# Row normalisation shared with GpSimd, 16-bit angles and filter loads ahead of the rows in a fused convolution and MLP kernel

## Chip, cores and metric

One core of a Trainium2 chip runs the kernel. The metric is the device time of one execution in microseconds (us). The span that a profile shows runs from the first to the last instruction and is some 2 us shorter. The runs come in a fast and a slow state; only fast runs are compared here. The granted clock is the share of TensorE's full clock that the chip allowed, 1.0 being all of it. Ratios are the mean time of one kernel's fast runs over that of the other's fast runs of the same rounds, so they differ a little from the ratio of the medians that are quoted.

## The reference, cut to what matters

```python
x = A_q                                          # (1, 2048, 640) bf16
g = sigmoid((x * gate_w).sum(-1))
# A: short causal convolution of k (4 taps per channel), times v,
#    then a convolution of length 2048 with ssm_k per channel through an FFT
kv = k_shift * v
y  = irfft(rfft(pad(kv)) * rfft(pad(ssm_k)))[:2048] + kv * ssm_D
a  = x * y
# B: row-normalised x, mixed over the rows by a two-layer MLP
h  = (x - mean(x)) / sqrt(var(x) + 1e-5)         # mean and var over the 640 channels
u  = gelu(einsum("bsd,sf->bdf", h, w1) + b1)
b  = (einsum("bdf,fs->bds", u, w2) + b2).transpose()
out = g * a + (1 - g) * b
```

## The kernel before: the parts that matter

The kernel turns the FFTs into products with sine tables on TensorE, in four residue classes of rows (`p` = 0 to 3), and mixes them by additions on VectorE. It does not issue its operations in the order of its text. It gives every operation an assumed duration, plans all engines with a list scheduler and emits each engine's operations in the planned order. An engine then takes its list strictly in that order.

```python
def ts(eng, o, a, s1, s2, op0, op1=None, mode=1, prio=None, extra=0.0):   # tensor_scalar
    n = n_of(o)
    d = dve_dur(n, mode) + extra if eng == "DVE" else n / 900.0 + 0.2     # GpSimd: 0.91 us for 640
    ...
def ln_scale(a, b):                       # 1/sqrt(var+eps) of tiles a..b-1, on GpSimd
    ts("POOL", sd[:, a:b], mv[:, a:b, 1], 1e-5, None, ALU.add, prio=0)
    tt("POOL", rstd[:, a:b], sd[:, a:b], V(cst, 1, [[0, n]]), ALU.pow, prio=0).dur = 1.05
    return tt("POOL", sd[:, a:b], sd[:, a:b], rstd[:, a:b], ALU.mult, prio=0)
def ln_apply(a, b):                       # (x - mean) * rstd in place, on VectorE
    for t in range(a, b):
        ts("DVE", xs, xs, mv[:, t, 0:1], rstd[:, t:t + 1], ALU.subtract, ALU.mult, mode=4, ...)
```

Here `ts` is an operation with one tensor and scalar operands, `tt` one with two tensors, `act` one of ScalarE. An evacuation copies TensorE's products out of PSUM, the memory where they land. I call `ln_scale` of tiles 0 to 7 the first scale and of tiles 8 to 15 the second.

A row tile is 128 rows of 640 channels. There are 16. TensorE's first MLP layer reads the normalised tiles; it serves as fill wherever the convolution makes TensorE wait. The order around the normalisation, the loads and the evacuation of the transposed filter were:

```python
for a, b in SSM0[:2]: ssm_load(0, a, b)          # filter blocks 0..3 of the first half
x_load(0)                                        # rows
ssm_load(0, *SSM0[2])                            # last filter block
for hk in range(1, 4): x_load(hk)
...
# filter block transposed on TensorE, D folded in by a 1-row matmul, evacuated by ScalarE
act(V(wT, ...), PSUM, ACT.Copy, name="wT")
...
for t in range(12): ln_tile(...)                 # statistics (bn_stats) on VectorE
ln_scale(0, 8);  ln_apply(0, 8)
for t in range(12, 16): ln_tile(...)             # after the first normalisations
ln_scale(8, 16); ln_apply(8, 16)
for g0 in KFP: tt("POOL", KF[...], cw, m32, ALU.mult)   # tap products, 4 pieces, on GpSimd
k_turn(0); k_turn(1)                             # reorder k (VectorE copies kp<-kn)
mixing(C[0], SS, 0)                              # first VectorE mixing of the filter spectrum
```

Of the kernel before, what the change touches and what calls it, by code (L numbers as in the profile page):

```python
# [9 lines left out]
BF16 = mybir.dt.bfloat16  # L10
F32 = mybir.dt.float32
I32 = mybir.dt.int32
ACT = mybir.ActivationFunctionType
# [5 lines left out]
class _Tracker:  # L19
# [31 lines left out]
    def regions(self, ap):  # L51
        name = ap.tensor.name
        info = self.mem.get(name)
        if info is None:
            return []
        space, base, rowsize, esize = info
        apl = [tuple(p) for p in ap.ap]
        esz_ap = mybir.dt.size(ap.dtype)
        assert esz_ap == esize, "bitcast size change unsupported in tracker"
        off = ap.offset  # L60
        assert isinstance(off, int)
        pstride, pcount = apl[0]
        if pcount > 1:
            assert pstride == rowsize, (name, apl, rowsize)
        p0 = off // rowsize
        rem = off % rowsize
        p1 = p0 + pcount
        assert p1 <= 128
        free = apl[1:]
        outer = free[:-1]  # L70
        inner = free[-1:] if free else []
        nouter = 1
        for st, ct in outer:
            nouter *= ct
        res = []
        if outer and nouter <= 64:
            idxs = [0] * len(outer)
            for _ in range(nouter):
                o = rem
                for (st, ct), i in zip(outer, idxs):  # L80
                    o += st * i
                lo = o
                hi = o
                for st, ct in inner:
                    ext = st * (ct - 1)
                    if ext < 0:
                        lo += ext
                    else:
                        hi += ext
                hi += 1  # L90
                assert lo >= 0 and hi <= rowsize, (name, apl, off, rowsize)
                res.append(self._reg(space, p0, p1, base + lo * esize, base + hi * esize))
                for d in range(len(outer) - 1, -1, -1):
                    idxs[d] += 1
                    if idxs[d] < outer[d][1]:
                        break
                    idxs[d] = 0
        else:
            lo = rem
            hi = rem  # L100
            for st, ct in free:
                ext = st * (ct - 1)
                if ext < 0:
                    lo += ext
                else:
                    hi += ext
            hi += 1
            assert lo >= 0 and hi <= rowsize, (name, apl, off, rowsize)
            res.append(self._reg(space, p0, p1, base + lo * esize, base + hi * esize))
        return res  # L110
# [172 lines left out]
    def mm(self, ps_ap, lhsT, rhs, start, stop, final_val, inc, transpose=False):  # L283
# [11 lines left out]
        ins = self.nc.tensor.matmul(ps_ap, lhsT=lhsT, rhs=rhs, start=start, stop=stop, skip_group_check=True)  # L295
# [30 lines left out]
class _Sched:  # L326
# [59 lines left out]
    def run(self):  # L386
# [13 lines left out]
        free = {e: 2.4 if e == "ACT" else 0.0 for e in engs}  # L400
        port = {"DVE": 0.0, "POOL": 0.0}
        dma_free = 0.0
# [109 lines left out]
def _build(nc, A_q, A_k, A_v, A_shift_k, A_ssm_k, A_ssm_D, B_x, B_w1, B_b1, B_w2, B_b2, gate_w, out):  # L512
# [10 lines left out]
    with ExitStack() as es:  # L523
# [61 lines left out]
        acol = alloc("acol", [128, 2, 4], I32, at=base_of(SS))  # L585
        brow = alloc("brow", [128, 2, 128], I32, at=base_of(SS) + 64)
# [9 lines left out]
        ksh = [alloc(f"ksh{i}", [128, 4, D], BF16, at=base_of(GT) + 5120 * (1 + i)) for i in range(2)]  # L596
        rows = alloc("rows", [20, 5, 512], BF16, at=base_of(GT))
        kn = [alloc(f"kn{i}", [128, 4, D], BF16, at=base_of(ring[1]) + 5120 * i) for i in range(2)]
        kp = [alloc("kp0", [128, NG, 128], BF16, at=base_of(ring[1]) + 10240), alloc("kp1", [128, NG, 128], BF16, at=base_of(GTB))]
        pint = alloc("pint", [128, 4, 2, 2, 256], I32, at=base_of(ring[1]))  # L600
# [83 lines left out]

        def memset(eng, ap, val, prio=None):
            return SC.add(eng, 0.2, lambda s: T.op(eng, lambda e: e.memset(ap, val), [], [ap]), [], [ap], prio=prio)  # L686
# [41 lines left out]

        def ssm_load(h, a, b):
            dma(ssm[:, a:b, 1024 * h:1024 * h + 1024], dr(A_ssm_k, 128 * S * a + 1024 * h, [[S, 128], [128 * S, b - a], [1, 1024]]), 128 * (b - a) * 2048, chain=True, rate=(262.0 if a == 0 else 195.0) if h == 0 else 385.0)  # L730
# [7 lines left out]
        def x_load(hk):  # L738
            dma(X[:, hk, :, :], dr(A_q, 512 * hk * D, [[4 * D, 128], [1, 4 * D]]), 128 * 5120, chain=True, rate=410.0)
# [30 lines left out]
        for a, b in SSM0[:2]:  # L770
            ssm_load(0, a, b)
        x_load(0)
        ssm_load(0, *SSM0[2])
# [11 lines left out]
        SPIN = (7, 3, 3, 2, 2)  # L785

        def spin(k):
            return [((lambda s: s[:, 0:512]), zz[:, 0:128], zz[:, :], True, True)] * k
# [4 lines left out]
        iota = lambda ap, pat, b, cm: SC.add("POOL", 0.2, lambda s: T.op("POOL", lambda e: e.iota(ap, pat, base=b, channel_multiplier=cm), [], [ap]), [], [ap])  # L793
        iota(dif[:, :], [[1, 128]], 0, -1)
        iota(acol[:, :, :], [[4, 2], [1, 4]], 0, 8)
        iota(brow[:, :, :], [[-512, 2], [4, 128]], 1, 0)
        iota(dif2[:, :], [[1, 32]], 128, -1)
        ts("DVE", ident[:, :], dif[:, :], 0.0, None, ALU.is_equal)
        memset("POOL", rows[0:20, 3:5, :].rearrange("g a b -> g (a b)")[:, 0:896], 0.0)
        ro, ri = V(rows, 1536, [[128, 4], [160, 4], [1, 32]], pn=20), V(rows, 0, [[1, 4], [0, 4], [4, 32]], pn=20)  # L800
        SC.add("DVE", 0.6, lambda s: T.op("DVE", lambda e: e.tensor_copy(ro, ri), [ri], [ro]), [ri], [ro], prio=0, name="taps")
        PORD = (0, 2, 1, 3)
        sins = {}
        for p in PORD:
            pv = pint[:, p, :, 1, :]
            t_ = tt("DVE", pv, V(acol, p, [[4, 2], [0, 256]]), V(brow, 0, [[0, 2], [1, 256]]), ALU.mult, mode=1)
            ts("DVE", pint[:, p, :, 0, :], pv, 1024.0, None, ALU.add, mode=2)
            pa = pint[:, p, :, :, :].rearrange("q a b c -> q (a b c)")
            if p != 0:
                t_.after.add(pprev)  # L810
            pprev = ts("DVE", pa, pa, 4095, None, ALU.bitwise_and, mode=2)
            pv3 = pa
            sins[p] = act(FTB[:, p, :, :, :, :].rearrange("q a b c d -> q (a b c d)"), pa, ACT.Sin, bias=cst[:, 0:1],
                scale=-(2.0 * math.pi / 4096.0) * (1.0 - 1e-6), name="sin")

# [24 lines left out]

        def transp(h, db):
            vt = _VT("cv")
            items = []
            for kt in range(2):
                for p in range(4):
                    o = (lambda s, j=4 * kt + p: s[:, 128 * j:128 * j + 128])
                    dfold = h == 0 and kt == 0 and p == 0
                    if dfold:
                        items.append((o, ident[0:1, :], Drow[0:1, 128 * db:128 * db + 128], True, False))
                    items.append((o, V(ssm, db * S + 1024 * h + 4 * kt + p, [[8, 128]]), ident[:, :], not dfold, True))  # L850
            m_ = mms(vt, (spin(SPIN[db]) if h == 0 else []) + items, name="wtr")
            m_.dur = 0.5
            o_ = act(V(wT, 2 * h * SL + 128 * db, [[SL, 2], [D, 4], [1, 128]]), (lambda s: s[:, :].rearrange("q (a b c) -> q a b c", a=2, b=4)), ACT.Copy, vt=vt, name="wT")
            if h == 0:
                o_.after.add(sins[0 if db == 0 else 2])
# [85 lines left out]
        MIXP = 330  # L941
        LNA = 8
        lnlast = []
        kfirst = []
        KFP = (0, 5, 10, 15)
        srcW = lambda h: (lambda kt, p, ci: wT[:, 2 * h + kt, p, 320 * ci:320 * ci + 320])
        for h in range(2):
            for db in range(ND):
                transp(h, db)
            if h == 0:  # L950
                consts()
            if h in (1,):
                fwd_even(srcW(h), h, C[h], 1.0 / 1024.0, h == 1, "W")
            for p in (PORD if h not in (1,) else PORD[2:]):
                if h == 0 and p in (1, 3):
                    sins[p].prio = SC.ops[-1].idx - (16.5 if p == 1 else 8.5)
                fwd(srcW(h), h, p, C[h], p, 1.0 / 1024.0, "W", (lambda c, k2: False) if h == 0 else (lambda c, k2: c == 1))
            if h == 0:
                for t in range(8):
                    ln_tile(t // 4, t % 4)  # L960
                for t in range(8, 12):
                    ln_tile(t // 4, t % 4)
                lnlast.append(SC.ops[-1])
                ln_scale(0, LNA)
                ln_apply(0, LNA)
                lnlast.append(SC.ops[-1])
                for t in range(12, 16):
                    for o_ in ln_tile(t // 4, t % 4):
                        o_.after.update(lnlast[-1:])
                ln_scale(LNA, 16)  # L970
                ln_apply(LNA, 16)
                lnlast.append(SC.ops[-1])
                for g0 in KFP:
                    tt("POOL", KF[:, g0:g0 + 20 // len(KFP), :, :], V(cw, 7 * g0, [[7, 20 // len(KFP)], [1, 7], [0, 32]]), V(m32, 0, [[0, 20 // len(KFP)], [0, 7], [1, 32]]), ALU.mult, xr=[pv3] if g0 == 0 else []).after.update(kfirst[:1])
# [344 lines left out]
```

## Time and profile before

| what | before |
|---|---|
| time, median of 3 (range) | 181.99 us (181.78 to 183.0) |
| span of the profiled run, granted clock | 179.7 us, 1.0 |
| first block of filter products on TensorE | 13.18 us |
| first MLP product on TensorE | 21.02 us |
| end of the last statistics on VectorE | 27.97 us |
| first mixing addition on VectorE | 32.94 us |

In later batches on other chips the kernel before took 181.98 to 182.46 us (medians of 7 to 11). In a timeline line the numbers are start, length, engine and kernel line; "x8" counts instructions run together; the bracket tells how long the engine was idle before it and what it waited for.

### The profile page before, as it was taken

To read this page: it belongs to the slowest core of one execution; us is meant where nothing else is said; L and a number is where in the kernel's file an instruction comes from. 1 tells how busy PE (TensorE), PEld (TensorE's weight loads), DVE (VectorE), ACT (ScalarE), POOL (GpSimd) and SP (SyncE) were. 2 spreads that over 40 slices of the span, in tenths; PEclk is the share of its full clock that TensorE was granted. 3 is DMA by queue.
4 is the path that set the end of the run, shared out by engine and by line. 5 is a ranking of instruction groups with operands and counts; after the bars stand their busy time and mean duration, and the time that the engine had idled before them with its cause. 6 is when DMAs were issued, how large, how long until landed. Compare 5 with 4: busy or idle time off the path is not lost.

```text
span 179.7 us, 3335 instructions
## 1 busy us (share of the span) xinstructions
PE 173.1 (96%) x1381; PEld 128.7 (72%) x1381; DVE 171.2 (95%) x203; ACT 116.9 (65%) x176; POOL 43.7 (24%) x42
## 2 busy tenths in 40 slices
PE   7969998899999999999999999999999999999993
PEld 2546785587778777776777778888888887777772
DVE  7999895999999999999999899999999999999984
ACT  5899998899898999617999932131231323753760
POOL 4089404190000054000240010402525000252000
PEclk9999999999999999999999999999999999999999
DMA  6999999999999999998299969797999999599463
GB/s 151 381 411 372 388 294 194 268 420 296 212 258 286 184 271 248 229 228 218 60 243 299 197 94 365 170 225 253 166 193 217 210 200 385 218 154 240 116 233 135
DMA packets 38542, 43.51 MB, mean 242 GB/s; under 512 B 15867, under 2 KB 31360, under 8 KB 38528
## 3 DMA queue, kind: packets, MB, share of 16 engines
q1 hardware_dynamic: 33296, 32.16, 58.2%
q0 software_dynamic: 5200, 11.14, 35.6%
q8 instruction: 11, 0.18, 0.4%
q14 instruction: 3, 0.02, 0.0%
q10 hardware_dynamic: 32, 0.01, 0.0%
HBM read 25.87 MB, written 2.62 MB: 159 GB/s over the span
## 4 chain that ended last, share of the span: by engine, by line
PE 88%; ACT 10%; DVE 0%; issue 0%
PE pp L295 88%; ACT wT L670 3%; ACT C L670 2%; ACT ksh L670 2%; ACT FTB L670 2%; ACT L670 1%; ACT GT L670 0%; DVE O L682 0%; DVE zz L686 0%; ACT cw L670 0%; DVE cst L686 0%
## 5 line engine op out<-in xcount | busy, mean ns | idle before, releaser
L295 PE MATMUL pp<-X,ring 128*128 128x320 bf16 x384 | 55.6, 299 | 0.0
L626 DVE TENSOR_TENSOR C<-C 128x2560 bf16<-128x2560 bf16 (+2 forms) x37 | 54.5, 1521 | 0.0
L295 PE MATMUL pp<-GT,W 128*128 128x320 bf16 x384 | 52.6, 299 | 0.0
L295 PEld LDWEIGHTS pp<-GT,W 128*128 128x128 bf16 x384 | 43.6, 114 | 8.6
L295 PEld LDWEIGHTS pp<-X,ring 128*128 128x128 bf16 x384 | 37.1, 98 | 14.9 <-DVE X L641 0.7
L670 ACT ACTIVATE C<-pp 128x640 bf16<-128x640 f32 x64 | 40.4, 723 | 4.9 <-PE pp L295 4.9
L670 ACT ACTIVATE O<-pp,c,omg 128x640 bf16<-128x640 f32 x15 | 13.3, 884 | 34.7 <-PE pp L295 34.7
L264 POOL DMA_DIRECT2D C<-C x8 | 10.9, 1610 | 41.7 <-DVE C L626 38.3
L295 PE MATMUL pp<-wT,FTB 128*128 128x320 bf16 x112 | 17.2, 299 | 2.5 <-ACT wT L670 1.4
L670 ACT ACTIVATE cgb<-pp,gg 128x640 bf16<-128x640 f32 x16 | 12.7, 794 | 5.7 <-PE pp L295 5.3
L295 PEld LDWEIGHTS pp<-wT,FTB 128*128 128x128 bf16 x112 | 10.5, 98 | 7.7 <-ACT wT L670 1.8
L670 ACT ACTIVATE GT<-pp,cc 128x640 bf16<-128x640 f32 x12 | 9.6, 799 | 9.0 <-PE pp L295 9.0
L626 DVE TENSOR_TENSOR tm<-C,C 128x2560 bf16<-128x2560 bf16 (+1 forms) x7 | 14.3, 2057 | 0.0
L922 DVE BATCH_NORM_STATS2 stats<-X 128x6 f32<-128x320 bf16 x32 | 13.5, 461 | 0.0
L295 PE MATMUL pp<-C,FTB 128*128 128x320 bf16 x96 | 13.4, 299 | 0.0
L264 POOL DMA_DIRECT2D C<-q_hi x6 | 5.9, 977 | 27.7 <-DVE C L626 13.2
L295 PEld LDWEIGHTS pp<-C,FTB 128*128 128x128 bf16 x96 | 9.3, 98 | 3.8 <-issue 0.3
L670 ACT ACTIVATE gq<-gq 128x640 bf16<-128x640 bf16 x16 | 11.8, 741 | 0.0
L626 DVE TENSOR_TENSOR SS<-C 128x2560 bf16<-128x2560 bf16 x8 | 11.7, 1487 | 0.1
L626 DVE TENSOR_TENSOR C<-tm 128x2560 bf16<-128x2560 bf16 (+1 forms) x9 | 10.6, 1192 | 0.1
L670 ACT ACTIVATE ksh<-pp 128x1024 bf16<-128x1024 f32 (+1 forms) x12 | 9.8, 894 | 0.6 <-PE pp L295 0.6
L670 ACT ACTIVATE wT<-pp 128x1024 bf16<-128x1024 f32 x10 | 9.7, 1041 | 0.6 <-PE pp L295 0.6
(73 smaller groups left out, 193.4 us busy)
## 6 DMA issues: line engine op xcount, KB each, us to landing
ring<-in_B_w_dram SPq DMA_DIRECT2D x12, 512.0 KB, 9.6
W<-in_B_w_dram SPq DMA_DIRECT2D x12, 512.0 KB, 6.5
C<-C POOLq DMA_DIRECT2D x8, 640.0 KB, 10.6
X<-in_A_q_dram SPq DMA_DIRECT2D x4, 640.0 KB, 8.4
kn<-in_A_k_dram SPq DMA_DIRECT2D x4, 640.0 KB, 9.3
out_dram<-O SPq DMA_DIRECT2D x7, 320.0 KB, 3.5
C<-SS POOLq DMA_DIRECT2D x3, 640.0 KB, 11.4
ssm<-in_A_ssm_k_dram SPq DMA_DIRECT2D x3, 512.0 KB, 6.8
```

Source lines behind the costliest of these rows:

```text
L264: ins = engobj.dma_start(out_ap, in_ap, accum_op=ALU.add, max_dma_last_dim=2560)
L295: ins = self.nc.tensor.matmul(ps_ap, lhsT=lhsT, rhs=rhs, start=start, stop=stop, skip_group_check=True)
L626: o_ = SC.add(eng, d, lambda s: T.op(eng, lambda e: e.tensor_tensor(o, a, b, op), rd, [o]), rd, [o], prio=prio, name="tt")
L670: return T.op("ACT", lambda e: e.activation(o, src, func, **kw), rr + [src], ww)
L922: ops.append(SC.add("DVE", 0.38, (lambda o, i: lambda s: T.op("DVE", lambda e: e.bn_stats(o, i), [i], [o]))(o, i), [i], [o]))
```

## The change

Its intent is to relieve VectorE ahead of the mixing and to start TensorE earlier. GpSimd takes five of the 16 normalisations; the sine tables' angles are made in 16 bits; three of the filter evacuations go to VectorE, out of 16-bit PSUM; the first-half filter products are made in column halves, so that they can start before the last filter blocks are in; all filter loads go ahead of the rows. All 16 statistics now stand in a row. The core of the diff (address setup, planner constants and the angle set-up are cut):

```diff
-for a, b in SSM0[:2]:
+for a, b in SSM0:
     ssm_load(0, a, b)
 x_load(0)
-ssm_load(0, *SSM0[2])
...
-    t_ = tt("DVE", pv, acol, brow, ALU.mult, mode=1)                     # 512 int32
-    ts("DVE", pint[:, p, :, 0, :], pv, 1024.0, None, ALU.add, mode=2)    # 512 int32
-    pprev = ts("DVE", pa, pa, 4095, None, ALU.bitwise_and, mode=2)       # 1024 int32
+    t_ = tt("DVE", pv, tb, jrow, ALU.add)                                # 1024 int16
+    pprev = ts("DVE", pa, pa, 4095, None, ALU.bitwise_and, mode=4)       # 1024 int16
...
-    items.append((o, ident[0:1, :], Drow[0:1, ...], True, False))        # D folded by a matmul
+    if (h, db) in ((0, 0), (0, 1), (0, 2)): evac_dve(o, i, vt, prio=0)   # 128x1024 bf16 PSUM
+    else: act(o, i, ACT.Copy, vt=vt, name="wT")
...
+    if h == 0 and db in (2, 4):                                          # D added to one row of wT
+        stt("DVE", o, o, 1.0, i, ALU.mult, ALU.add, prio=0)              # 1x320, two SBUF inputs
...
+    for ci in range(2):
+        for p in PORD:
+            fwd_c(p, ci, C[0], 1.0 / 1024.0)                             # column halves
...
+    for t in range(16):
+        ln_tile(t // 4, t % 4)
+        if t == LNA - 1: ln_scale(0, LNA)
     ln_scale(LNA, 16)
+    PAP = tuple(range(5))
+    for t in PAP:
+        ts("POOL", xs, xs, mv[:, t, 0:1], rstd[:, t:t + 1], ALU.subtract, ALU.mult, prio=0)
+    for t in range(16):
+        if t not in PAP: ln_apply(t, t + 1)
-    tt("POOL", KF..., xr=[pv3] if g0 == 0 else [])                       # waited for the angles
+    tt("POOL", KF...)
```

## The prediction

> **What bounds the kernel now.** I read the busy table and the 40 slices first, because a kernel with two engines above 90% can't be judged from one of them.
>
> ```profile
> PE 173.1 (96%) x1381; PEld 128.7 (72%) x1381; DVE 171.2 (95%) x203; ACT 116.9 (65%) x176; POOL 43.7 (24%) x42
> ```
>
> TensorE and VectorE are both nearly full, so the end moves only if both gain. The table of windows, cut where TensorE starts to be full, shows where either could:
>
> ```profile
> 0.00:13.18 13.18, 10.53 (x74) 5.28 (x74) 12.19 (x34) 10.40 (x11) 5.53 (x12) 1.00 0.86 312
> 13.18:29.58 16.40, 16.40 (x144) 12.41 (x144) 14.16 (x44) 14.48 (x22) 8.29 (x8) 1.00 1.04 329
> 29.58:40.93 11.35, 10.03 (x118) 7.02 (x116) 10.85 (x15) 10.44 (x15) 5.63 (x3) 1.00 1.02 321
> 40.93:177.06 136.13, 136.11 (x1048) 104.00 (x1048) 133.44 (x111) 81.61 (x129) 24.29 (x21) 1.00 0.94 221
> ```
>
> Columns are length, then busy time of PE, PEld, DVE, ACT, POOL. From 40.93 on TensorE never rests and VectorE rests 2.7 us in 136. What can be won lies before 40.93 us.
>
> The timeline of VectorE shows its pauses there:
>
> ```profile
> 19.95 2.94 DVE L641 TENSOR_SCALAR X<-X,mv,rstd 128x640 bf16<-128x640 bf16 x8 [0.57 <-POOL rstd L626]
> ...
> 30.08 2.94 DVE L641 TENSOR_SCALAR X<-X,mv,rstd 128x640 bf16<-128x640 bf16 x8 [2.11 <-POOL rstd L626]
> 32.94 1.49 DVE L626 TENSOR_TENSOR SS<-C 128x2560 bf16<-128x2560 bf16 x1
> ```
>
> Both wait for GpSimd's power that makes the inverse deviations. The mixing of the filter spectrum starts at 32.94, and from there to the last combination VectorE has a fixed list of operations.
>
> The timelines near the end show which engine gates the finish:
>
> ```profile
> 146.22 5.69 DVE L626 TENSOR_TENSOR C<-C 128x2560 bf16<-128x2560 bf16 x4
> 151.94 1.49 DVE L626 TENSOR_TENSOR C<-C,C 128x2560 bf16<-128x2560 bf16 x1
> ```
> ```profile
> 150.68 8.86 PE L295 MATMUL pp<-C,FTB 128*128 128x320 bf16 x64
> 159.37 5.60 PE L295 MATMUL pp<-GT,W 128*128 128x320 bf16 x40
> 164.93 4.51 PE L295 MATMUL pp<-C,FTB 128*128 128x320 bf16 x32
> 169.27 4.51 PE L295 MATMUL pp<-SS,FTB 128*128 128x320 bf16 x32
> 173.62 3.42 PE L295 MATMUL pp<-GT,W 128*128 128x320 bf16 x24
> ```
>
> The inverse transforms (<-C,FTB and <-SS,FTB) start as soon as VectorE has combined a slot: the third of the four additions from 146.22 ends near 150.5, and the transform starts at 150.68. The second inverse starts at 164.93, after the first of two additions from 163.30. Between them TensorE fills in with layer-two products (<-GT,W). So although the chain of waits gives 88% to TensorE, the finish hangs on VectorE as well. If only TensorE were early, it would run out of fill: second inverse done at 173.6, ScalarE 0.9, VectorE's last products, additions and two 0.55 us operations, about 177.1 against 177.6 now. TensorE alone can win about 0.5 us at the end.
>
> **What the Trainium skill says.** "VectorE: DVE Perf Modes", "The perf-mode tier table": copy and tensor_scalar reach 4x on 16-bit data in SBUF and at most 2x from PSUM; tensor_tensor 2x on 16-bit and 1x on 32-bit. The trace agrees: a 128x2560 bf16 tensor_tensor takes 1485 ns, the 2560-element copy into kp 811, the 512-element int32 multiplication 684. No 16-bit PSUM read is in this trace.
>
> "SBUF — State Buffer", "Who interferes with whom": VectorE in a 2-port mode and GpSimd hold a shared port pair in turn, whoever starts first, for a whole instruction; two SBUF inputs on VectorE contend with a GpSimd operation that reads. The trace agrees: GpSimd's copy of 20 elements per partition at 35.27 takes 4.96 us, under back-to-back tensor_tensors.
>
> "GPSIMD Engine Reference", "4.1 Engine selection": one-input work on GpSimd is roughly line-rate. The nearest row is a two-input one, 1120 elements in 2060 ns, so 640 elements at about 1.0 to 1.2 us is an estimate.
>
> "TensorE: Matmul & The Clock Gate", "Part 1": about 3.4 us of sustained work come before the full clock. The trace agrees: the first seven filler matmuls take 3.14 us, 0.45 each, the next three 0.81.
>
> **The change part by part.**
>
> *Angles.* Now four rounds on VectorE of a 512 int32 multiplication (start to start 0.61), an addition (0.36) and a mask on 1024 int32 (0.60): 1.57 each, 6.3 in all. New: a set-up of 128-element product, mask and addition, about 0.6, then four rounds of a 1024-element 16-bit addition (2x: 0.61, from 1.40 per 2560) and mask (4x: 0.33, from 0.73 per 2560): 3.76. Sum 4.4, saving 1.9. GpSimd pays with eight more iotas of 0.3, otherwise idle.
>
> *Row tiles.* Five of 16 normalisations at 0.36 start to start leave VectorE: 1.8 saved; some 5.5 us on GpSimd.
>
> *Filter blocks by VectorE.* Three evacuations of 1024 bf16 from PSUM at 2x, an estimated 0.62: 1.9 added. ScalarE loses three at 0.94: 2.8 saved there. The fold of D by 1-row matmuls becomes two additions on one partition, 320 elements, 0.4 each: 0.8 added. A memset moved from GpSimd adds 0.5.
>
> VectorE's work: -1.9 - 1.8 + 1.9 + 0.8 + 0.5 = -0.5 us. The two transfers cancel; nearly all the change does for VectorE's work is move it.
>
> *Pauses.* Today 0.57 + 2.11 = 2.7 us. New order: all 16 statistics in a row, scale of tiles 0 to 7 meanwhile, so the first pause goes. The second scale still waits for the last statistics: the chain took 2.1 us (28.0 to 30.08). Meanwhile VectorE could normalise tiles 5 to 7 (1.1) and turn a k tile (0.73), but those are 2-port operations, and the power (1.66), or a fill still running on GpSimd, holds the pair. I leave 1.0 to 1.5. Pauses saved: 1.2 to 1.7.
>
> VectorE reaches the mixing at 32.94 - 0.5 - 1.5, near 31.0: 2.0 us earlier.
>
> *Filter loads first and column halves.* Filter products now start at 13.18. Of the 13.18 us the needed work is 40 transposes at 0.07, 0.25 of constants and one product: 3.1, so 10.1 are lost; between 29.58 and 40.93 some 2.1 more (12 + 24 products at 0.136 and 4.33 of convolution taps). New: at 280 GB/s from 2.0 us (the windows show 282 and 284 GB/s there) the first 0.79 MB land near 4.9, say 5.4. Two groups of transposes at 0.55 and two evacuations at 0.62, partly overlapped, put the first product near 7.5. That is 5.7 earlier, but ScalarE then paces: 16 evacuations at 0.6 against 0.54 on TensorE, plus two blocks at 0.94 and two late sines. The last of these filter evacuations ends near 20.4 instead of 24.03. TensorE's gain: 3.5 to 5.
>
> The X rows land later: 1.97 MB by about 8.0 to 8.5 us, from the windows' rates. VectorE is busy with angles, evacuations and set-up until about 10, so this costs nothing.
>
> *Sum.* The finish gains the smaller of TensorE's 3.5 to 5 and VectorE's 2.0 plus up to 0.5 at the tail: 2.4. Start-up and landing of the output stay. 182.0 - 2.4 = 179.6 us.
>
> **The rivals.**
>
> *A. TensorE is the real bound.* The chain of waits speaks for it. Then the full 3.5 to 5 comes: 177 to 178.5. Against it stand VectorE's 95% and the inverses that start within 0.2 us of its additions.
>
> *B. The lock eats the pause.* If GpSimd's five tiles run into the second scale, VectorE waits over 2.5 us again and its copies are blocked besides. Then only the 0.5 us of work and the 0.5 at the tail remain: 181. For it: the 4.96 us copy. Against: most of GpSimd's tiles fall under the statistics, which take one input and no 2-port mode.
>
> *C. A late transfer.* The k loads keep their place behind filters, rows and weights, so the turned k can't be much earlier than now. VectorE took the first gated product at 40.01, when ScalarE's first evacuations of ksh had just ended. If VectorE is 2 us early there and ScalarE isn't, it waits, and the gain falls to 0.5 to 1: 181 to 181.5. ScalarE's own gain of about 3.6 speaks against.
>
> *D. Slower modes.* If 16-bit additions ran at 1x, 1.8 us more; if evacuations from PSUM did, 1.4 more. Both together: 182 to 183.
>
> **Range and chances.** My point is the smaller-of-two sum. A puts the low end at 178.0, B and C the high end at 181.4. Over 2% needs 3.6 us, that is VectorE with hardly a pause left, or rival A: 0.20. Slower by 2% would need D and a cold clock together: 0.02. The rest, 0.78, is within 2%.
>
> **What would show each step.** The first filter product near 7.5 us and the last filter evacuation near 20.4; 16-bit additions near 0.69 us and masks near 0.4 in the groups; block evacuations on VectorE near 0.7; GpSimd's tiles near 1.1 each; a pause of 1 to 1.5 us for rstd; the mixing at about 31; VectorE's busy time about 170.7; the inverses still starting right behind VectorE's additions. A mixing start at 29 or earlier, or an end that follows TensorE's gain and not VectorE's, would prove me wrong, as would pauses of VectorE between 30 and 45 us.

## The result, and the profile after

The changed kernel took 191.68 us (191.3 to 192.07, 4 runs) against 181.96 (181.78 to 183.0, 4 runs): ratio 1.0522, 95% interval 1.0474 to 1.0569. It is slower by 9.7 us; the span grew by 10.2, from 179.7 to 189.9. The prediction of 179.6 and its range missed it altogether.

The busy table of the changed kernel, in answer to the first one of the prediction:

```profile
PE 173.2 (91%) x1363; PEld 128.7 (68%) x1363; DVE 173.9 (92%) x203; ACT 114.4 (60%) x173; POOL 54.9 (29%) x54
```

TensorE has the same busy time and fewer instructions (fewer filler matmuls, which do no needed work, but products at half clock, as shown below). The growth of the span is idle time. The table of windows with the prediction's cuts (length, then busy PE, PEld, DVE, ACT, POOL, then granted clock) shows where it lies:

```profile
0.00:13.18 13.18, 10.21 (x74) 6.13 (x74) 11.40 (x29) 9.00 (x11) 8.08 (x19) 1.00 0.86 322
13.18:29.58 16.40, 10.20 (x87) 6.70 (x85) 16.37 (x48) 12.17 (x20) 12.80 (x9) 0.85 0.91 301
29.58:40.93 11.35, 6.81 (x34) 3.71 (x34) 2.91 (x8) 3.33 (x5) 9.70 (x7) 0.61 1.03 292
40.93:189.90 148.97, 146.02 (x1173) 112.17 (x1170) 143.18 (x121) 89.86 (x140) 24.30 (x21) 1.00 0.88 208
```

Between 29.58 and 40.93 VectorE worked 2.9 of 11.4 us (10.85 before) and TensorE ran 34 matmuls (118 before, 80 of them the short tap products) at a mean clock of 0.61. After 40.93 TensorE again hardly rests, but it has 1173 instructions left where it had 1048. The timeline of VectorE there:

```profile
28.92 1.51 DVE L649 TENSOR_SCALAR X<-X,mv,rstd 128x640 bf16<-128x640 bf16 x3
38.87 2.94 DVE L649 TENSOR_SCALAR X<-X,mv,rstd 128x640 bf16<-128x640 bf16 x8 [8.44 <-POOL rstd L634]
41.72 0.82 DVE L634 TENSOR_TENSOR C<-C 128x1280 bf16<-128x1280 bf16 x1
```

It is done with its statistics at 29, normalises the three tiles that it may, and waits 8.44 us for the second scale. The mixing starts at 41.72 instead of 32.94. GpSimd's timeline says why the scale is late:

```profile
21.02 0.25 POOL L648 TENSOR_SCALAR sd<-mv 128x8 f32<-128x8 f32 x1 [3.43 <-DVE mv L968]
...
23.31 13.54 POOL L649 TENSOR_SCALAR X<-X,mv,rstd 128x640 bf16<-128x640 bf16 x5
36.83 0.25 POOL L648 TENSOR_SCALAR sd<-mv 128x8 f32<-128x8 f32 x1
37.16 1.67 POOL L634 TENSOR_TENSOR rstd<-sd,cst 128x8 f32<-128x8 f32 x1
```

The five row tiles take 13.5 us, and the second scale, whose input was ready at 29.0, stands behind them in GpSimd's list. Their own line (duration least, median, most in ns; first and last start):

```profile
L649 POOL TENSOR_SCALAR X<-X,mv,rstd x5: 2497/2514/3257, 23.3 to 34.4; 128x640 bf16<-128x640 bf16 x5
```

The last two tiles ran from 31.87 to 36.85, while VectorE was idle, and took 2.50 us each; so the ports that GpSimd shares with VectorE do not make this length. Tiles two and three, beside VectorE's copies and normalisations, took 3.26 and 2.82.

TensorE suffers from the same tiles directly:

```profile
25.92 0.69 PE L298 MATMUL pp<-X,ring 128*128 128x320 bf16 x2 [3.47 <-POOL X L649]
29.13 0.71 PE L298 MATMUL pp<-X,ring 128*128 128x320 bf16 x2 [2.51 <-POOL X L649]
31.93 0.71 PE L298 MATMUL pp<-X,ring 128*128 128x320 bf16 x2 [2.09 <-POOL X L649]
34.42 0.72 PE L298 MATMUL pp<-X,ring 128*128 128x320 bf16 x2 [1.77 <-POOL X L649]
```

It gets two products for each tile and waits for the next, 9.84 us in four waits, and takes nothing else meanwhile, though transposes of the second filter half stand behind these products. The clock row of the 40 slices (tenths of full speed, 4.75 us each) shows that these short bursts did not keep the clock up. In a finer cut it stood at 0.50 from 25 to 38 us, the last 3 us of it without a pause of TensorE:

```profile
PEclk9999965599999999999999999999999999999999
```

The end of the kernel shows which of the two engines is behind. The timelines of TensorE and of VectorE near the second inverse:

```profile
169.67 5.60 PE L298 MATMUL pp<-GT,W 128*128 128x320 bf16 x40
175.10 4.51 PE L298 MATMUL pp<-C,FTB 128*128 128x320 bf16 x32
```
```profile
172.86 2.89 DVE L634 TENSOR_TENSOR C<-SS 128x2560 bf16<-128x2560 bf16 x2
```

The first of VectorE's two additions ends near 174.3, the inverse begins at 175.10, when TensorE's fill ends. VectorE is 0.8 us ahead (0.15 before); TensorE is the later one.

**An account for comparing the runs.** From 41 us on TensorE rests 2.7 to 4.9 us in nearly every kernel, so its end depends on how much needed work it has behind it by then. I count that work at full pace: the products started before 41.0 us in the timeline, 0.136 us for one of 320 columns (before: 40 in 5.61 us and 15 in 2.21, so 25 in 3.40), 0.054 for a tap product (80 in 4.33), 0.067 for each of the 80 filter transposes. Filler matmuls count nothing. Before it is 137 products, 80 tap products and the transposes: 28.3 us; after, 94 products and the transposes: 18.1. The loss of 10.2 is the growth of the span to the tenth. The needed work is the same in every kernel (1104 products, 160 tap products, 80 transposes), so this is close to bookkeeping: the sum changes only with how long TensorE rests after 41 us. It tells where time was lost, not why. The table has every run, of fast runs alone; "by 41" is this work, and the sum should be near 208 where nothing further is lost after 41 us.

| run | time, us (range, runs) | ratio to before [95%] | span | by 41 | sum |
|---|---|---|---|---|---|
| before | 181.96 (181.78 to 183.0, 4) | | 179.7 | 28.3 | 208.0 |
| after | 191.68 (191.3 to 192.07, 4) | 1.0522 [1.0474, 1.0569] | 189.9 | 18.1 | 208.0 |
| e1 | 184.57 (183.98 to 185.24, 4) | 1.0159 [1.0134, 1.0183] | 181.7 | 27.4 | 209.1 |
| e2 | 191.64 (191.4 to 193.11, 4) | 1.0552 [1.0511, 1.0592] | 189.6 | 21.0 | 210.6 |
| e3 | 185.62 (184.84 to 186.1, 4) | 1.0200 [1.0172, 1.0228] | 183.7 | 24.6 | 208.3 |
| e5 | 183.11 (182.77 to 183.53, 4) | 1.0043 [1.0000, 1.0087] | 180.4 | 28.3 | 208.7 |
| e6 | 186.11 (185.36 to 186.24, 4) | 1.0198 [1.0153, 1.0243] | 183.9 | 24.5 | 208.4 |
| e7 | 186.28 (184.42 to 186.47, 3) | 1.0165 [1.0079, 1.0251] | 184.1 | 24.5 | 208.6 |
| e8 | 185.86 (185.56 to 187.19, 4) | 1.0207 [1.0152, 1.0262] | 184.8 | 24.5 | 209.3 |
| e9 | 199.50 (197.78 to 200.68, 3) | 1.0989 [1.0924, 1.1053] | 195.4 | 24.4 | 219.8 |
| e10 | 192.64 (191.1 to 192.95, 3) | 1.0542 [1.0472, 1.0612] | 190.7 | 21.6 | 212.3 |
| e11 | 184.95 (184.94 to 185.04, 4) | 1.0144 [1.0096, 1.0193] | 182.7 | 27.2 | 209.9 |
| e12 | 184.73 (184.12 to 184.93, 4) | 1.0125 [1.0081, 1.0169] | 182.5 | 27.6 | 210.1 |
| e13 | 184.23 (183.82 to 184.29, 4) | 1.0114 [1.0098, 1.0131] | 182.1 | 28.0 | 210.1 |
| e14 | 185.22 (184.93 to 185.52, 4) | 1.0179 [1.0161, 1.0197] | 182.8 | 27.3 | 210.1 |
| e15 | 183.45 (183.33 to 183.91, 4) | 1.0081 [1.0063, 1.0099] | 181.1 | 27.1 | 208.2 |
| e16 | 182.25 (182.19 to 182.31, 4) | 1.0011 [0.9996, 1.0026] | 180.4 | 28.0 | 208.4 |
| e17 | 182.11 (181.76 to 182.36, 6) | 0.9997 [0.9963, 1.0032] | 180.2 | 27.5 | 207.7 |
| e18 | 182.95 (182.33 to 183.13, 6) | 1.0038 [0.9999, 1.0076] | 181.1 | 27.2 | 208.3 |

e4 has one execution only and a wrong result, and is told below.

### The profile page after: what moved, and what is told of

Same layout as the page of the kernel before. It is cut to its first block, busy times and chain, and to the rows that moved or that the text cites. A ratio compares the mean times of both kernels' runs of the same rounds, so it can differ in the third digit from the quotient of the medians.

```text
span 189.9 us, 3310 instructions
## 1 busy us (share of the span) xinstructions
PE 173.2 (91%) x1363; PEld 128.7 (68%) x1363; DVE 173.9 (92%) x203; ACT 114.4 (60%) x173; POOL 54.9 (29%) x54
## 4 chain that ended last, share of the span: by engine, by line
PE 79%; DVE 8%; POOL 7%; ACT 2%; DMA 2%; issue 1%
PE pp L298 79%; POOL X L649 6%; DVE stats L964 3%; DVE wT L658 2%; ACT C L678 2%; DMA ssm<-in_A_ssm_k_dram 2%; POOL rstd L634 1%; DVE wT L684 1%; DVE pint L634 1%; DVE pint L648 1%; DVE mv L968 0%; ACT GT L678 0%; DVE O L690 0%; DVE rows L838 0%; POOL sd L648 0%
## 5 line engine op out<-in xcount | busy, mean ns | idle before, releaser
L298 PE MATMUL pp<-X,ring 128*128 128x320 bf16 x384 | 58.0, 306 | 10.1 <-POOL X L649 9.8
L298 PEld LDWEIGHTS pp<-wT,FTB 128*128 128x128 bf16 x112 | 10.2, 99 | 7.7 <-ACT C L678 2.5
L267 POOL DMA_DIRECT2D C<-q_hi x6 | 5.9, 977 | 27.4 <-DVE q_hi L634 10.1
L649 POOL TENSOR_SCALAR X<-X,mv,rstd 128x640 bf16<-128x640 bf16 x5 | 13.5, 2718 | 0.0
L678 ACT ACTIVATE wT<-pp 128x1024 bf16<-128x1024 bf16 x7 | 6.9, 1141 | 10.7 <-PE pp L298 10.7
L649 DVE TENSOR_SCALAR X<-X,mv,rstd 128x640 bf16<-128x640 bf16 x11 | 4.4, 474 | 8.4 <-POOL rstd L634 8.4
```

The costliest lines, as they stand in the source:

```text
L267: ins = engobj.dma_start(out_ap, in_ap, accum_op=ALU.add, max_dma_last_dim=2560)
L298: ins = self.nc.tensor.matmul(ps_ap, lhsT=lhsT, rhs=rhs, start=start, stop=stop, skip_group_check=True, is_transpose=True if ps_ap.dtype = ...
L649: return e.tensor_scalar(o, a, s1, s2, op0=op0, op1=op1)
L678: return T.op("ACT", lambda e: e.activation(o, src, func, **kw), rr + [src], ww)
```

## The experiments

Theory at the start: the five tiles on GpSimd make nearly the whole loss, since one takes 2.5 us and the second scale stands behind them. Rival: the loss lies in the rest (locked additions of D, order, loads), and the tiles only fill a wait that would be there anyway.

### e1: the change without GpSimd's tiles

```diff
-        PAP = tuple(range(5))
+        PAP = ()
```

> The changed kernel with one edit: all 16 row tiles are normalised by VectorE, none by GpSimd. Theory 1 (the five GpSimd tiles, 2.5 us each, stand in GpSimd's queue ahead of the second scale and hold back VectorE and TensorE): the 8.44 us wait for rstd falls to about 2, VectorE does 1.8 us more, its mixing starts near 36 instead of 41.7, and the time is 185 to 187. Theory 2 (another part of the change, such as the new load order or the column halves, costs most of the 10 us): still above 189.

Measured: 184.57, a little better than expected. VectorE now normalises all 16 tiles without a wait:

```profile
28.80 5.74 DVE L649 TENSOR_SCALAR X<-X,mv,rstd 128x640 bf16<-128x640 bf16 x16
34.46 2.95 DVE L634 TENSOR_TENSOR C<-C 128x1280 bf16<-128x1280 bf16 x3
```

The tiles cost 7.1 of the 9.7 us, and 9.2 (before rounding) of the 10.2 us of TensorE's work by 41. But what is left of the change is still 2.6 us slower than the kernel before. A side result: GpSimd's power ran under these 16 two-port normalisations, took 2.00 us instead of 1.68, and the normalisations ran at 0.36 us each, no slower than before. The pause of 1.0 to 1.5 us that the prediction allowed for a lock did not come.

### e2: the kernel before with GpSimd's tiles alone

```diff
+                if t in PAP:        # PAP = (0, 1, 2, 3, 4)
+                    ts("POOL", xs, xs, mv[:, t, 0:1], rstd[:, t:t + 1], ALU.subtract, ALU.mult, prio=0)
+                    continue
```

> The kernel before with only the five GpSimd tiles added and nothing else of the change. Theory 1: GpSimd is busy with them from about 20.2 to 33, the second scale follows and ends near 35 instead of 30, VectorE's wait grows by about 5, and the time is 186 to 189. Theory 2: the tiles alone are harmless, 181 to 183.

Measured: 191.64, above the range. The tiles alone cost the kernel before as much as the whole change does, with the same wait:

```profile
35.47 2.94 DVE L641 TENSOR_SCALAR X<-X,mv,rstd 128x640 bf16<-128x640 bf16 x8 [8.43 <-POOL rstd L626]
```

### e3: two tiles instead of five

```diff
-        PAP = tuple(range(5))
+        PAP = (0, 1)
```

> The changed kernel with two GpSimd tiles instead of five. Theory 1 (a queue ahead of the second scale): two tiles end near 28.4, before the last statistics at 29, so the second scale isn't held, and the time is that of the kernel without GpSimd tiles or up to 1 us better, 184 to 187. Rival (each GpSimd tile costs VectorE a fixed share through the shared ports): two fifths of the loss stay, some 2.5 us above the kernel without them.

Measured: 185.62, and VectorE has hardly a wait for the scale (0.14 us): the two tiles ran from 23.24 to 29.0, just to the end of the statistics. So the cost isn't so much per tile. Up to the two tiles that fit under the statistics the scale isn't held up; the other three cost 6.1 us together. But the two tiles gain nothing either: the time is 1.0 us above e1 in the medians (0.4% in the ratios, whose intervals overlap; e1's one run at the clock of e3's, 0.981, took 185.24). TensorE waited 1.68 us for the second tile.

### e4: one operation in the tile instead of two

```diff
-    ts("POOL", xs, xs, mv[:, t, 0:1], rstd[:, t:t + 1], ALU.subtract, ALU.mult, prio=0)
+    ts("POOL", xs, xs, mv[:, t, 0:1], None, ALU.subtract, prio=0)
```

> The changed kernel with each GpSimd tile reduced to the subtraction, the multiplication left out (the numbers are wrong on purpose). If GpSimd pays by scalar operation, a tile takes about 1.3 to 1.6 us, VectorE's wait falls from 8.4 to 3 or 4, and the time is near 186 to 187. If it pays by element moved, a tile stays at 2.5 and the time at 191 to 192.

Measured, one run of unknown state: 184.4 us. The edit had a second effect that I had not thought of: without the scale as an input the tiles ran at 13 to 23 us, ahead of everything. So its time says nothing on the question, and only the duration counts:

```profile
L648 POOL TENSOR_SCALAR X<-X,mv x5: 1872/1873/2204, 13.2 to 21.0; 128x640 bf16<-128x640 bf16 x5
```

A tile with one operation takes 1.87 us, with two 2.51, which is between the two expectations. Dropping an operation would not bring it near the 1.1 of the prediction.

### e5: e1, and the tap products kept off the additions of D

The two additions of D took 1.68 and 2.31 us in the changed kernel, on one partition, while GpSimd made the tap products KF. Here the first piece of KF waits for both additions (it is given a read of the row that they write).

```diff
-    tt("POOL", KF..., ALU.mult)
+    tt("POOL", KF..., ALU.mult, xr=[V(wT, 320, [[1, 320]], pn=1)] if g0 == 0 else [])
```

> No GpSimd tiles, and the build of KF on GpSimd now waits until both additions of D on VectorE are done. Theory 1: those additions, with two inputs in SBUF, waited for GpSimd's KF pieces (1.68 and 2.32 us instead of about 0.4). Alone they take 0.4 to 0.5 each, VectorE's mixing starts near 31.3 instead of 34.46, and the time falls by about 3, to 181 to 182.5. Rival (VectorE's early gain is given back later, because TensorE or ScalarE sets the end): mixing earlier, time still 184 to 185.

Measured: 183.11, better than e1 by 1.5 us in the medians, by 1.3 in the spans, by 1.2% in the ratios (the two ran in different batches, on different chips). The medians of the runs at a mean clock of 0.991, three of each, differ by 1.0 us. The additions take 0.48 and 0.46 us, so the lock is shown. The two lines of the changed kernel, then those of e5:

```profile
9.69 1.68 DVE L658 SCALAR_TENSOR_TENSOR wT<-wT,Drow 1x320 bf16<-1x320 bf16 x1
13.35 2.31 DVE L658 SCALAR_TENSOR_TENSOR wT<-wT,Drow 1x320 bf16<-1x320 bf16 x1
```
```profile
9.67 0.48 DVE L658 SCALAR_TENSOR_TENSOR wT<-wT,Drow 1x320 bf16<-1x320 bf16 x1
12.13 0.46 DVE L658 SCALAR_TENSOR_TENSOR wT<-wT,Drow 1x320 bf16<-1x320 bf16 x1
```

The mixing starts at 31.52, 2.9 us earlier than in e1 and 1.4 earlier than before. But the time is not better than before. TensorE shows where the gain was given back; e5 first, then the kernel before:

```profile
24.47 0.31 PE L298 MATMUL pp<-wT,FTB 128*128 128x320 bf16 x1 [1.13 <-ACT wT L678]
26.30 2.15 PE L298 MATMUL pp<-wT,FTB 128*128 128x320 bf16 x11 [1.52 <-ACT wT L678]
28.69 1.25 PE L298 MATMUL pp<-X,ring 128*128 128x320 bf16 x8 [0.24 <-ACT C L678]
```
```profile
21.02 1.25 PE L295 MATMUL pp<-X,ring 128*128 128x320 bf16 x8
```

TensorE started its filter products 3.4 us earlier (9.79 against 13.18) and was done with the first half at 20, but had no fill after it: no row tile is normalised before 25.86, since all statistics come first, and the second half waits for ScalarE. From 20 to 30 us it was busy 6.76 us, 9.84 before. By 41 us it had done the same 28.3 us of work. VectorE then waited 1.61 us for a k tile to land at 40, which is the prediction's rival C.

### e6, e7, e8: e5 with one further part undone each

e6 gives the three filter evacuations back to ScalarE, e7 puts the row load back between the filter loads, e8 makes the filter products in whole rows.

```diff
# e6
-        WTD = ((0, 0), (0, 1), (0, 2))
+        WTD = ()
# e7
-        for a, b in SSM0:
+        for a, b in SSM0[:2]:
             ssm_load(0, a, b)
         x_load(0)
+        ssm_load(0, *SSM0[2])
# e8
-                for ci in range(2):
-                    for p in PORD: fwd_c(p, ci, C[0], 1.0 / 1024.0)
-            for p in (() if h == 0 else PORD[2:]):
+            for p in (PORD if h == 0 else PORD[2:]):
```

> As e5_kf_after_d, and ScalarE evacuates all five filter blocks (no VectorE evacuation from bf16 PSUM). If VectorE's total work sets the end, 1.8 us less on VectorE give 179.5 to 181. If ScalarE paces the early stage, its 2.8 us more delay the filter products, and the time is that of e5_kf_after_d or up to 2 us longer.

> As e5_kf_after_d, with the first row load back between the filter loads as before the change. If the load order is worth little because VectorE is busy until about 10 us anyway: within 1 us of e5_kf_after_d. If the early filter blocks matter: 1 to 2 us longer.

> As e5_kf_after_d, with the filter products in whole rows that need all five blocks, as before the change, instead of column halves. TensorE starts its first product near 12 us instead of 9.7. If VectorE sets the end: within 1 us of e5_kf_after_d. If TensorE's early start counts: about 2 us longer.

Measured: 186.11, 186.28 and 185.86, some 3 us slower than e5 each, more than expected of any. In the profiled runs of all three the granted clock falls in the windows 20 to 30 and 30 to 41 us (to 0.91 and 0.93 in e6, 0.79 and 0.88 in e7, 0.93 and 0.91 in e8), and TensorE has 24.5 us of work by 41.

Part of the 3 us goes with that clock, and not all of it with the edits. e5's profiled run, which stays at 1.00 in these windows, was its fastest and the only one of its four with a mean clock of 1.00 (the others had 0.991). e7 alone took 184.42 us at 1.00 and 186.28 and 186.47 at 0.981, with the same program. Runs with about the same mean clock compared, e7 is 1.7 us slower than e5, e6 2.1 and e8 2.4 (few runs each). TensorE's pauses between 22 and 30 us, 1.1 and 1.5 us for ScalarE, stand in all four profiles, so they alone do not say why the clock fell in one and not in another; that stays open. How much of the rest is the part itself and how much the new plan around it, these runs don't tell.

### e9: the last five tiles on GpSimd, behind the second scale

```diff
-        PAP = tuple(range(5))
+        PAP = tuple(range(11, 16))
```

> The changed kernel, but GpSimd takes the last five row tiles (11 to 15) and not the first five, so its second scale stands ahead of them in its queue and not behind. The wait of VectorE for the scale (8.44 us in the changed kernel) should fall under 0.5 us, if the queue made it; the five tiles should still take 2.5 us each (12.5 in all), and since they start only at about 30 us, TensorE should wait for them until about 43. Theory that VectorE's wait is what sets the end: 185 to 187, near the 184.57 of the kernel without these tiles. Rival, that TensorE's wait for tiles of X (it takes its work in order, and drops to half clock) costs as much by itself: 189 to 192.

Measured: 199.50, worse than both theories. VectorE's wait for the scale is gone (mixing at 32.65), and yet the time is the longest of all. My first theory, that VectorE's wait for the scale is what costs, falls in this form. The tiles ran beside VectorE's two-input mixing and slowed from 2.50 us to up to 5.03:

```profile
L649 POOL TENSOR_SCALAR X<-X,mv,rstd x5: 2497/3973/5030, 31.7 to 47.3; 128x640 bf16<-128x640 bf16 x5
```

TensorE waited for each in turn, with the next 20 filter products behind them:

```profile
42.36 0.71 PE L298 MATMUL pp<-X,ring 128*128 128x320 bf16 x2 [1.96 <-POOL X L649]
47.38 0.72 PE L298 MATMUL pp<-X,ring 128*128 128x320 bf16 x2 [4.30 <-POOL X L649]
50.87 0.71 PE L298 MATMUL pp<-X,ring 128*128 128x320 bf16 x2 [2.77 <-POOL X L649]
51.37 5.06 PE L298 MATMUL pp<-wT,FTB 128*128 128x320 bf16 x20
```

ScalarE was then idle 9.90 us for TensorE and VectorE 9.05 us for ScalarE. So a slow tile in front of TensorE was enough here, without VectorE's wait for the scale.

### e10: the changed kernel with the plan told the tile's duration

```diff
-    ts("POOL", xs, xs, ..., ALU.subtract, ALU.mult, prio=0)
+    ts("POOL", xs, xs, ..., ALU.subtract, ALU.mult, prio=0).dur = 2.6
```

> The changed kernel, where only the figure in its own plan for a GpSimd row tile is changed, from 0.91 to 2.6 us; no operation is added or removed, only their order. In this plan the second scale still stands behind the five tiles, but TensorE's order is made for late tiles. VectorE's wait for the scale should stay at 7 to 9 us, TensorE's waits for tiles should nearly go and its granted clock stay near 1 between 20 and 40 us. Theory that VectorE's wait sets the end: 189 to 191.5, little better than the changed kernel's 191.68. Rival, that TensorE's stall in order is the larger half: 185 to 187.5.

Measured: 192.64, 1.1 above the theory's range; the rival's 185 to 187.5 falls. TensorE's waits for tiles sank from 9.84 to 3.74 us and it had 3.4 us more work done by 41. VectorE's wait stayed:

```profile
39.01 0.80 DVE L649 TENSOR_SCALAR X<-X,mv,rstd 128x640 bf16<-128x640 bf16 x2 [7.02 <-POOL rstd L634]
```

The work gained by 41 us was lost after it: TensorE rested 6.5 us from 41 us on (2.95 after the change), 5.65 of them at the very end, where the new plan had left no MLP product to cover the last evacuations and additions. With e9 this speaks for the tiles holding up both engines, so that freeing one leaves the other late. It is argued and not shown: both edits moved the whole plan.

### e11: e5 with half of the tiles normalised early

```diff
                     if t == LNA - 1:
                         ln_scale(0, LNA)
+                        ln_apply(0, LNA)
```

> The changed kernel without GpSimd's tiles and with the tap products behind the two additions of D (183.11 before), and now VectorE normalises tiles 0 to 7 right behind the first scale, as in the kernel before, and tiles 8 to 15 after the statistics. Theory that the rest of the loss is TensorE's late fill (its first layer-one product at 28.7 us against 21.0): first such product at 22 to 24, mixing at 31.5 to 32.5, time 181 to 182.5. Rival, that the rest is ScalarE's pace and the late k tile, which this leaves alone: 183 to 184.

Measured: 184.95, above both ranges. The first MLP product came at 23.56 as hoped, but the rest did not follow: the statistics that now come after the first normalisations put a wait of 1.56 us for the second scale back, and TensorE waited for row tiles and for ScalarE in smaller pieces. Its work by 41 was 27.2, less than in e5. The theory that only the late fill was missing falls.

### e12, e13: the 16-bit angles alone, and with two sines moved

e12 is the kernel before with the angle part of the change (and the memset of the taps' rows on VectorE). e13 adds:

```diff
                 o_.after.add(sins[0 if db == 0 else 2])
+                if db == ND - 1:
+                    for p in (1, 3): sins[p].after.add(o_)     # late sines behind the last filter evacuation
```

> The kernel before with the 16-bit angles alone (the memset of the taps' rows on VectorE, the other parts as before). VectorE's angles should fall from about 6.3 to 4.4 us. If VectorE's work ahead of the mixing sets the end, 180.3 to 181.2; if TensorE's stream and the filter loads set it, since VectorE's saved time only becomes waits, 181.7 to 182.8. The share of the prediction that the angles carried (1.4 to 1.9 us) is read from this.

> The angles alone (184.73), with the two late sines made to follow ScalarE's last filter evacuation. In the run of the angles alone they stood ahead of the last two evacuations and the first block of filter products began at 14.35 us against 13.18 in the kernel before. If that order made the loss: last filter evacuation 1 us earlier, first block at 13.0 to 13.4, time 182 to 183. Rival, that VectorE's new waits (for the scale and for k, 4.5 us in all) made it: 184 to 185, unchanged.

Measured: 184.73, above both ranges, and 184.23, in the rival's. VectorE's busy time fell by 1.2 us, from 171.2 to 170.0, but its idle time grew by more: it waited 1.30 us (e12) and 1.86 us (e13) for the k tile near 22 and 0.8 and 0.5 for ScalarE in the mixing, which it did not before (the 2.12 us for the second scale are no new wait, they were 2.11), which began at 34.12 and 34.03, later than before. Moving the sines brought the first block of filter products from 14.35 to 12.20, as meant. The time is half a microsecond lower in the medians, but the intervals of the two ratios overlap. The rival, the new waits, fits the rest: the saved work alone is worth less than nothing in these orders.

### e14, e15: e13 with the filter loads first, then with a middle order of statistics

```diff
# e14: as the loads of the change
# e15, on e14 (and e16, on the kernel before):
-    for t in range(12): ln_tile(...)
-    ln_scale(0, 8); ln_apply(0, 8)
-    for t in range(12, 16): ln_tile(...)
-    ln_scale(8, 16); ln_apply(8, 16)
+    for t in range(14): ln_tile(...)          # first scale behind tile 7; KF's last piece behind that
+    ln_apply(0, 4)
+    for t in range(14, 16): ln_tile(...)
+    ln_scale(8, 16); ln_apply(4, 16)
```

> The last kernel, and all filter loads ahead of the rows. The last evacuation should then no longer wait for the last filter block; first block of products at 11.6 to 12.4. If TensorE's start sets the end, 1 us less than the last kernel: 181 to 182. Rival, that VectorE sets it (the statistics start later with the rows): no gain, 182 to 184.

> The last kernel, and a middle way for the statistics: 14 tiles' statistics, four normalised tiles, the last two statistics, then the other normalisations, and the fourth piece of the tap products behind the first scale. VectorE's pauses for both scales should be under 0.5 us each, mixing at 30 to 31.5 us and first layer-one products by 24. If VectorE's pauses set the end: 179.5 to 181.3, faster than the kernel before. Rival, that the filter products and the late k tile pace what follows: 181.5 to 183.

Measured: 185.22 and 183.45. With the loads first the filter products began at 12.44, not earlier than in e13, and VectorE waited 2.6 us for the rows: a loss of 1 us, so the rival (no gain) was even too kind. The middle order won 1.8 back and has the mixing at 31.86, with a pause of 0.85 us left for the second scale, but is still 1.5 us behind the kernel before.

### e16: the middle order of statistics in the kernel before

> The kernel before with that order of statistics alone. It takes away the pauses of 0.57 and 2.11 us and adds no work. If VectorE's arrival at the mixing sets the end: mixing at 30.5 to 31.5 and time 180 to 181.2. Rival, that the time saved turns into waits for ScalarE or for the k tile: 181.5 to 182.6.

Measured: 182.25 against 181.98, ratio 1.0011 [0.9996, 1.0026]: no gain. The pause of 2.11 us became 0.84, and the mixing began 1.43 us earlier:

```profile
28.65 2.94 DVE L641 TENSOR_SCALAR X<-X,mv,rstd 128x640 bf16<-128x640 bf16 x8 [0.84 <-POOL rstd L626]
31.51 1.49 DVE L626 TENSOR_TENSOR SS<-C 128x2560 bf16<-128x2560 bf16 x1
```

TensorE had 28.0 us of work by 41, 0.3 less than before. VectorE's idle time from 41 us on rose from 4.8 to 6.4 us. An earlier VectorE bought nothing here; but TensorE's first block of filter products also came 0.45 us later (13.63), so the edit did not move VectorE alone.

### e17, e18: the sines moved in the kernel before, without and with the middle order

The edit is that of e13, in the kernel before (e17) and in e16 (e18).

> The kernel before with the two late sines behind ScalarE's last filter evacuation, nothing else. First block of filter products at 12.2 to 12.6 us against 13.18. The account that TensorE's work done by 41 us sets the end (span of the profiled run plus that work was 208.0 us before, 208.0 after the change, 208.4 with the order of statistics alone): whatever this run has done by 41 us, its span should be 208.0 to 208.8 less that work. If the earlier products are kept until 41 us: 29 us of work and a time of 181.2 to 181.7. Rival, that ScalarE's sines then stand ahead of the products' evacuations and the gain is gone by 41 us: work 28 to 28.4, time 181.8 to 182.6.

> The same and the order of statistics of the run without the scale pauses. VectorE is early at the mixing (31 to 31.6 us) as well. If the early TensorE start and VectorE's early mixing add up: 180.5 to 181.4. If TensorE's work by 41 us alone counts, 208.0 to 208.8 less that work for the span, and with work near 28.3 a time of 181.8 to 182.5.

Measured: e17 182.11 (same as before), e18 182.95. The first block came at 12.75 and 13.09, so 0.4 and 0.1 earlier than before only, later than expected. e18's span of 181.1 plus its work of 27.2 is 208.3, in the range set ahead. e17's sum is 207.7, 0.3 under it. As the needed work is fixed, this tests only that TensorE's rest after 41 us stays near 3 us. The rival's side was right in e17: the early products were used up by 41 us (27.5, even less than the 28 to 28.4 expected). No version that I ran beats the kernel before.

## Why the prediction was wrong

**The tile on GpSimd, "about 1.0 to 1.2 us", is the step that failed first.** It was an estimate from the row of a two-input product over 1120 elements in 2060 ns, scaled to 640. The tile took 2.5 to 3.3 us, 2.7 on average. Five of them are 13.5 us and not "some 5.5". The first scale ended at 23.3: five tiles of 1.1 would have ended at 28.8, just with the statistics at 29.0, as I had it ("most of GpSimd's tiles fall under the statistics"). Five of 2.7 end at 36.8. The plan in the kernel assumed 0.91 and went wrong in the same way, though telling it 2.6 (e10) did not win the time back. e2 shows that this part alone costs 9.7 us, e1 that leaving it out gives 7.1 back.

**"I leave 1.0 to 1.5" for the pause.** It was 8.44. I looked for a lock between the power and VectorE's copies; e1 shows that there was none worth speaking of. What counted was the place in GpSimd's list, behind the tiles.

**"VectorE reaches the mixing at ... near 31.0."** It was 41.72, 8.8 us late instead of 2.0 early. With tiles and lock taken out (e5) it was 31.52. That this is near 31.0 is partly luck: e5 does 1.8 us more normalising than the sum and has no pause where the sum left 1.0 to 1.5. With both put in, the sum gives 32.94 + 1.3 - 2.7 = 31.5, so its other terms were right.

**"TensorE's gain: 3.5 to 5".** It was a loss of 10.2 us of work by 41. For the tiles' share the reason is in the four waits and the half clock. For the rest, e5 shows a gain of nothing: the first products came at 9.8 and not 7.5, ScalarE paced them as foreseen (last evacuation near 21.7, 20.4 predicted), and the 3.4 us won there were idle time between 20 and 30. I had counted the early start and not asked what TensorE would do when it ran out of filter products before any row was normalised.

**"two additions on one partition, 320 elements, 0.4 each".** They took 1.68 and 2.31 under GpSimd's tap products, 3.2 us too much on VectorE; VectorE's total of 173.9 is 3.2 above the predicted 170.7, just that. e5 puts the cost at 1.0 to 2.2 us of time, by what is compared.

**The rule "the finish gains the smaller of" the two engines' gains** agrees with what was measured once the sizes are put right: after the change TensorE is the later engine by 0.8 us at the second inverse, and the span grew by its loss. e5 and e16 agree as well: VectorE gained 1.4 in each, TensorE nothing, and the finish nothing. But the reading on which the rule rests was not shown. "The inverse transforms start as soon as VectorE has combined a slot": in the kernel before, VectorE's additions ended at 150.50 and 164.78 and the inverses began at 150.68 and 164.93, and TensorE came to both from its fill without a pause. It was the later engine there too, if only by 0.2 us.

**The rivals.** Rival A, that TensorE is the real bound, fits these runs as well as the rule does; they can't be told apart, since in no run did TensorE have more work done by 41 us than before. Rival B had the right direction and half the mechanism (the tiles run into the second scale), but sized it as a wait of "over 2.5 us" and 181 us of time. Rival C occurred in e5 (1.61 us for the k tile). Rival D did not: 16-bit additions took 0.68, masks 0.41, evacuations from 16-bit PSUM 0.67 to 0.69, all as predicted. The chance of 0.02 for a loss of over 2% was tied to rival D together with a cold clock. The clock did go cold, but from the tiles, which that line did not name.

**What stays open.** Why the smaller parts, without the tiles, come out at or above the time before in every combination tried is known only as far as the account goes: TensorE has no more work behind it by 41 us. In e12 to e14 TensorE also rests 4.4 to 4.9 us after 41, and not 2.7 as before; in e12 the last MLP fill has 12 products where it had 24, but why the plan spends its fill earlier was not followed up. Nor was the clock, which differs between fast runs of one kernel and moved the time by up to 2 us (e7). Every edit also moves the planned order of all engines, so none of these runs changes one thing only.

## What to carry to other kernels

Before work is moved to an idle engine, measure one instruction of exactly that kind and size there, and ask what stands behind it in that engine's list and what in-order consumers stand in front of it; an engine that is 24% busy can still be the one that everybody waits for. An earlier start is a gain only if the engine has other ready work when it gets through with it. Where a kernel plans its own order from assumed durations, a wrong one is built into the order of every engine; but putting that one figure right (e10) gained nothing here, since the slow work still stood in the way.

## What the Trainium skill lacked or had wrong

- "GPSIMD Engine Reference", section "4.1 Engine selection", has one-input elementwise work on GpSimd at roughly line rate. Here a 128x640 bf16 tensor_scalar with two per-partition scalars took 2.50 us at best, with VectorE idle (3.9 ns per element), and 1.87 with one operation, against 0.36 start to start on VectorE, nearly seven times as long. Per element that is twice its own two-input product, 1120 elements in 2.06 us (1.8 ns). The page has no figure for this form.
- "SBUF — State Buffer", section "Who interferes with whom", says that the loser of the shared ports blocks for a whole instruction. Under GpSimd's two-input products it agrees: VectorE's two-input additions of 320 elements on one partition took 1.68 and 2.31 us, each to 0.34 us after the end of the product that had started before it, and 0.46 to 0.48 without; VectorE's 2560-element copies took 1.62 and 1.92 us under such products (e4). Under GpSimd's one-input tiles it doesn't agree. The same copies took 0.80 us inside a tile in the changed kernel; in e4 the second addition began 0.06 us after a tile and took 0.46 us; in e9 three VectorE instructions that began inside the tile from 42.29 to 47.32 took 1.47, 0.81 and 2.00 us (1.48, 0.81 and 1.48 elsewhere), and it was the tile that grew, from 2.50 to 5.03 us.
- The same section doesn't tell how a GpSimd instruction with little data fares: the power on 8 elements per partition only went from 1.68 to 2.00 us under 16 back-to-back normalisations (e1), which lost nothing.
